# A spectral filter's time transform split as 128 by 16 points instead of 64 by 32, its middle matmuls in smaller array tiles

## The chip, the cores and the metric

The kernel runs on one core of a Trainium2 chip. The metric is the device time of one execution in microseconds (us); the figure given is the median of several runs. The engines are PE (TensorE matmul, with PEld its weight loads), DVE (VectorE), ACT (ScalarE), POOL (GpSimd) and SP (SyncE, which only issues transfers here).

## What is computed

The reference applies two blocks, and then both again. Block A normalises each row, takes a two-dimensional real Fourier transform over 2048 times and 512 features, multiplies it by a complex filter, transforms back and adds the input. Block B normalises, multiplies by two weight matrices, multiplies the two products elementwise, multiplies by a third matrix and adds the input.

```python
def _A_ref(x, w_r, w_i):
    X = rfft2(x, axes=(-2, -1))
    X = X * (w_r + 1j * w_i)
    return irfft2(X, s=(S, D), axes=(-2, -1))
def _B_ref(x, w_gate, w_up, w_down):
    return ((x @ w_gate) * (x @ w_up)) @ w_down
x = x + _A_ref(_layernorm(x), A_w_r, A_w_i)
x = x + _B_ref(_layernorm(x), B_w_gate, B_w_up, B_w_down)
```
The last two lines run twice: B=1, S=2048, D=512, F=1792.

## The kernel before, in words

The input lies in SBUF as `xs`, 128 partitions by 16 tiles by 512 features. Each of the two layers has three stages.

**Forward transform** (`fwd_rest`, from L459). Each of the 16 tiles is folded over the features, and four float32 matmuls into a PSUM bank `tp` do the long part of the time transform together with its twiddle factors (`tw`, from the constant `tf`). With 64 by 32 points a tile holds two of the 32 short indices, 64 rows each, so that half of every `tw` is zeros. ACT (or ACT and DVE) copies `tp` to `E`, which holds 4 blocks by 16 tiles by 16 groups by 8.

**Middle** (`middles`, L519, and `middle`, L549). The loop over `TWOS` (L1010) takes the 16 groups of frequencies in turn. For every group:
- `fs`: the sum and the difference of two halves of `E`, on POOL (on DVE for groups 0 and 1);
- `dp`: the transform over the features, 8 matmuls, each with 64 stationary columns of `fs` and 128 moving columns of `df`, written to one or the other half of the PSUM partitions; two groups share one planned step;
- `zs`: an ACT copy of `dp` to SBUF;
- `zp`: the short part of the time transform, 2 matmuls (4 in group 0) over all 128 partitions with 64 columns of a constant (`f2`, `f20`) each, and 512 moving columns;
- the filter, a complex product. Even groups go way "1": two ACT instructions put the swapped halves of `zp` in `jz`, DVE multiplies `zp`, POOL multiplies `jz`, DVE adds them to `ys`. Odd groups go way "2": four DVE instructions, with the swapped product in a PSUM bank `qp`;
- `vq`: the short part backward, 8 matmuls, each with 64 columns of `ys` stationary and 128 columns of a constant moving;
- an ACT copy of `vq` back into `E`.

**Inverse and product stages.** `inv` (L590) reads all 16 groups of `E`: its first matmuls `yi` wait for the last of these copies. Then the rows are normalised, turned and split into high and low parts (`build_x`), and the matmuls of block B (`gx`, `gw`, ..., `db`, `ex`, ...) follow.

Float32 matmuls leave two matmul and two weight load records each. The routine `halves` (L317) is what places two matmuls in the two column halves of the array:

```python
def halves(o, a, b):
    for c in (slice(0, 64), slice(64, 128)):
        TE.matmul(o[c], a[:, c], b, start=True, stop=True, skip_group_check=True)
```

The order on every engine is written out: `Plan.op` records each step with its engine, an assumed pitch and what it reads and writes, and `Plan.order` (L257) replays the steps in the order packed in the string `ORDER`, with places in the buffer rings from `PLACES`. Each engine runs its steps strictly in that order. All instructions are recorded through the queue wrapper, at L303. PSUM has eight banks: rings "x", "y", "w" of one, "a" of three and "d" of two (L224); SBUF temporaries such as `zs`, `jz` and `ys` share the ring "f" of 18. Before the middle and after it `idle` (L514) issues one 512-column matmul `wp` that nothing reads.

Of the kernel before, what the change touches and what calls it, by code (L numbers as in the profile page):

```python
# [14 lines left out]
ALU = mybir.AluOpType  # L15
# [13 lines left out]
def consts():  # L29
# [19 lines left out]
    j, p, q = np.arange(32), np.arange(64), np.arange(32)  # L49
    c, s = _cs(q[:, None, None] * (32 * p[None, :, None] + j[None, None, :]), 2048)  # L50
# [4 lines left out]
    tf = np.zeros((2, 64, 16, 16, 2, 2, 2))  # L55
    ti = np.zeros((64, 2, 16, 2, 64))
    for jj in range(2):
        tf[jj, :, :, :, :, jj] = f.reshape(16, 2, 2, 64, 16, 2)[..., jj].transpose(3, 4, 0, 2, 1)
        ti[:, jj, :, jj] = g.reshape(64, 64, 16, 2)[..., jj].transpose(0, 2, 1)
    w = np.exp(-2j * np.pi * (np.outer(j, j) % 32) / 32)  # L60
    late = np.exp(-1j * np.pi * j / 32)[:, None] * w
    unit = np.array([1.0, 1j])
    fs, gs = [], []
    for special in (False, True):
        z = np.zeros((2, 2, 32, 2, 32), complex)
        y = np.zeros((2, 2, 32, 2, 2, 32))
# [7 lines left out]
        fs.append(np.stack([z.real, z.imag], 3).reshape(2, 2, 16, 2, 128).transpose(0, 2, 1, 3, 4).reshape(128, 128))  # L74
# [10 lines left out]
        gs.append(y.reshape(128, 2, 2, 16, 2).transpose(0, 1, 3, 2, 4).reshape(128, 128) / 2048)  # L85
    mid = np.concatenate([*fs, *gs], 1).astype(np.float32)
# [16 lines left out]
SWAPS = "12" * 8, "12" * 8  # L103
FAST = (0, 1)
CUTS = {g: ((0, 12), (12, 16)) for g in range(3)}
TWOS = [(0,)] + [(g, g + 1) for g in range(1, 15, 2)] + [(15,)]
# [10 lines left out]
    'c-l=`2Y3}#)1GtgO%Dkz5a|*+ibyp<igZMpNReW}f_zf^M35>dRT2FJ73?4&iV#phP(Tncbiqc6h#(y)0YV5#_RRmz>?ZzCp1pVP*;A*y^UiFDqNzMZQ68V<+vq%(p|f0)u5m2g#C6UjIzus'  # L117
    '(NQVC8YG}W~<){RmV1t%QxUTaRu8i+%Xi30ajx)Iwe&6IuxX<Gl++V=6V)(p^)^aqJvYF%xEZPgW3dK=1Doy7&9y64{h+SNpLYV0kTg+XKEP7SOo(z?vEBLfnV;QH|G?&H0sVy_lH`81U)un'
    'j4f%zQHVbM$0Er}7w`C0s0hLL44uR#m5d{?FeTmy4E?7uWcqNOx`W%G3|jybkq4(94q5xc6Q>;BAlWByo3p$5fbrsI4KJ?qkT^t>G_T;lRNe-=m5LF~IcBw)~UKiAjx9h^*`VeNPt4JjvL#S'
    'pcot1P=@UaRZ1r{$bvpaZNG#&1h|&{lv^W%x4Hp}9N)t#9Mp=XfPQh*>@U6H<$zT%5vEGMV5{WMJqXT)*pGEHqr1e&Xgh+d8fa87{}lX%uVIJz04K`iM@W@Wj$@{3u<7WUg{e8o?9v{066dj'  # L120
    'yKXmoi7J_s)O&^lpgxsv3JA`rEOdfmSLbdS?>d$uBVHq!}xqc_feYu;-ipi9`0vAFTMqppaERK??HmM<J8yr63fXOQEQ$?rLf=U`5jn~fy52X<2P}41{PKV`@CQGGFK%f`jhWi+J}A(agz4D'
    '4O%mLdU=vUr`hN@hFyw956ABxcqdNN88*SZ3~lA<N3_;bJ2QHv@zeNx4A&(*Igjg3)w9ey*t`$_=!f6CSfu@jn`#DgY2F!X2DM#O30-y<s4477)?LHWcPIPfJE*R9K+gB5loHjxrLDBt$*EM'
    'Fc0&URXuE^t$$TAcpvQ(-dppZct6|;?cy@(5>a!3e_6>gozsli#u>OZA9jks$W1OXl<{%%z7^fc4m-?y{+F@Vf6P01#&1fjkN83{L5+4{upRn|nS=#{x;#CWgG@WN+#R$3u-#icPdEA4tRol'
    'b0|8(`nZFqK-k74CD@IC|i@8TSeRJ;8Ot9I4<bofO>d{>9|dvLBIMh~i~GHr`qL-{*8in%vnw@snN2e>~hH=R6pks5Lz^h;ph>a*w=iv(`RZkOua(~xxxP8QZR53$JpaasTm`UUORAfb)e=_'
    'fkgLay?;h*I>7`S9E(^d^slO+vHmYvwhY0~?N^dUP4B3-~#Vc$1^3xypV!r&CY97i$^l>=G{_=SEOnJD$3Di+CKpj`n8g`Jn4=U&Z}g9t$sd2jeY0kGtaNVQCaBYAW}F_Zw=AS@(O7*-<POU'
    'PAYh5LkRe-EoY`H#1F?H=$rFy<|3ErW$;JAE8;mYlmOgToi>&UrvXX1R2E+4{=?L&&B-?ubE}O<{~kxf#=^zd1$T0g7ya~3iJPp>zo^GzQ*@`be^_)Einb!xFSYWpfdET8)ME=8U9DDcfNP8'
    'ZHfCi-hVB00{{4h%Nj#9@a%j18bIH{J4^EgoU9V>(Q}2&89eDj!(AsU{$=40k?bhMtmt}_Z@Cy#jwK2;G@{3*l;igC8ux;Y0`kn|H*J;|hZSz4vKY77g{cMB+y_rLz><?Li82vs#8wWHc%D@'
    'mKIE;i+t8yMpXW$(Ol`Lc_4FRJ(NvFrr5R?Sxe8CdSNmshk{?6daaeaeJwzGsQj0w??}g<)NtuXVhgtTq8|M*y);8ivGTRj@iIwUbSvMW~yWgBsyQ&KNw2C|i=$b~UYFWOI%3lJ_=EigiUKF'
# [12 lines left out]
    'sRNdYb>NQ7QOxlp6%<_1Mig{qts?%k!Ov>_f&m4o^H4hIOR0`HIDj&&x$0XfY`FS#JdQU=SG&SKT&i4gFJ}}T!fKKuLI^Ti^v#P6!+S}W|pzw&q`&P*R?|6dr}mgb)}8us^3FfZ87EmTK~b-'
    '7P}MaYzuNY`D}nO)s!bS-~*U_8jW?Ynkjt4#hXGayp9~qM;XZ_-hlu8<GLF^>v#MMkB58=&UFTP%L97qaagsl3#ng}pxI`z`->*fYuo{zk)!hc+&yPj;%)-@jAOl?t39ny4jf7IT{qK7SI^`'
    '9e3B*mDW<3IK;I!V8wNHcBffM!O#&@*A0oQ1<GIw?r3CwKqvx&**;+_h<RhMVH}ca&$SXvCJ|DufG3@jIY?i3I)OE!SaWsZ}c5mPtvw_Ur%xbqK(BgPlsX>odk!`HfYRzTX`q%J?ii$OYJeG'
    'R9uZ<x87MA)>qGsj|fv&#B{Mfgjo9S*Jb|-Y-Va>Kr2eugvZJy-8?u_yEzC}mLS!Tl*cNbYi9nEaSt`h>^i-9MGgIYyZpkyu8d{}J+RsyCF4%o^p&8!NM=NE41TH9Md#5duG23gn!mOL-dt8'
    'b0QioNJRI<Sl_iVHs|dtArAdiPl0Z~oyjwAPzww{lA`sXOgv^k`iat9B|!mb}eJ&8@Jg@<^=CsEi`11>##N>?uN@rhBDqNO$Ucr0*g1wW=Uo$^boO_xmyX4Q4M+`NdXnbiaONky9Fa1X;WEe'
    '^BRG!M&k}Mw%ha@yc1hK4GX%Ad^G<tk-~sSwWs0oIg?bUP(WH5BP$Q2(^G5sev@4_VPFK#Ea0v4)#$-B%T7ipXe>YDo1o|gtlaARb(0+E0CzP8Bf<L7R$_;q9d(fh+iFKsSh<)PKP~$O&qe3'
    '%7g!aUkK)Afx$Kc>y*9M#Q0X2>lD{g-`a&fwPA0aFmAp59eeAD85?;&*xq>dH{Vb3-T|C63{MLKO)|j3cjMZiavtpMv@x{bG=MiJ!}1Csn=EK2nl?hWKg0Ip@Rtu15Dt*bR|>!faF!KjGpzG'
    '0cHh}cgZ=%>*d>CCWrtPLQMht6_c^LIa#<^znOa$>PChc03Tk)p`YF=s2`!xFazJdE<40)VPcG!%=Mc9fLp{V&#rqprA$dt0l~nc<6Cj_jy$}#Ua*<+19{C$swX}c3etvz4n^3yR@;brZWcF'
    '0L0-LxctcnMzz9oO$Zz{T2_{u17qK@!~XtmDn8XxY(98&wOr4?OaRl*bedd49x2@P#4%1$GdO(r3G9*w;856HPxQ0J09n>FT~)>vKzXq7;IrE;Ij>av~^kxsGRzdx>QM`FUy{Hx|Y6|`czhI'
    '<9pl%%L6m>~?YcYr$GfU%4-CIdfr<GYZRv<dt}80@0pewx-#{O9Wf--r!<rv~+5tE*(eqB4;AXW^2uB9C_z>7;fd&#nR~Q>AK!-_P;W%3{O7)ozf|E&c|QZ$|QaH1eruuyzwNihS|VZ5T4#q'  # L150
    '!{Pneh};_1ldHvVtt;niDiz5;jdvt!dTN7-nkE`ZAdD=tH3Fhn^0p~t-f0U2pghDwbDJFUI7X`Vw^jQ9A__2;y19P6_TkU63l?~AH;nxTEgv2bDqxW@N^5l9HyCC<4M%)+rVeuP|N6tcu)n`'
    '?TFxCWA-{MdwvhQeH=XS2uEwJ?iMtb1G^FKd7jq;S&l;2A>_ppdoysB7pX1}&=cfyU#$m9jU<ZvD(-Cj`UJoFOT9qr6L-K~_NtEVfhCCc7IQyXom0z-L*JHanH@E&T*^1JPbxfV7Z7O@{fBx'
# [120 lines left out]
def kernel(ctx: ExitStack, tc: tile.TileContext, x, wf, wc, wb, dfwd, tf, ti, mid, out):  # L273
# [245 lines left out]
    def middles(gs, E, df, W, due, swaps):  # L519
# [26 lines left out]
        for g, dp in zip(gs, dps):  # L546
            middle(g, dp, E, W, due(g), swaps[g])
# [620 lines left out]
```

## Time and profile before

| | |
|---|---|
| median of 3 runs | 1038.42 us (1037.62 to 1038.68) |
| the profiled execution's own time | 1037.49 us |
| its span | 1035.7 us |
| PE busy | 1020.6 us (99%) |
| DVE busy | 793.7 us (77%) |
| POOL busy | 745.8 us (72%) |
| ACT busy | 419.7 us (41%) |

The span is what the profiler saw from the first to the last instruction; the execution's own time is 1.8 us longer. Busy time is a sum over the whole span, and the stages differ: the profile by windows and the chain of waits tell which engine sets the pace in each.

### The profile page before, as it was taken

Reading aid. Unit: us, or ns where it says so; the run is one execution under the profiler, and the core shown is the slowest. Engines: PE = TensorE matmul, PEld = TensorE weight load, DVE = VectorE, ACT = ScalarE, POOL = GpSimd, SP = SyncE. Lnnn points to the kernel's source line nnn. Section 1 sums busy time; section 2 is a strip of 40 time slices with the busy share of each in tenths; the row PEclk is TensorE's granted clock in tenths of the full one; section 3 lists DMA queues with packets and bytes.
Section 4 is the critical chain, followed back from the end, with each engine's and each line's share of the span. In section 5 each row is a group of like instructions: output and inputs, shape, how many; then the busy total and the mean of one; then the engine's idle time right before and its main releaser. Section 6 shows DMA issues by size and latency. Waiting matters only on the chain.

```text
span 1035.7 us, 18681 instructions
## 1 busy us (share of the span) xinstructions
PE 1020.6 (99%) x6544; PEld 878.8 (85%) x6544; DVE 793.7 (77%) x1533; ACT 419.7 (41%) x989; POOL 745.8 (72%) x950
## 2 busy tenths in 40 slices
PE   8999999999999999999999999999999999999998
PEld 6777988888888888889987789888888888888897
DVE  7779777678866677778878796888887766677788
ACT  6679534434432422332376693222333421222231
POOL 6968999999997675655798466554779953456571
PEclk9999999999999999999999999999999999999999
DMA  9720677767785675455290005536796365565442
GB/s 346 304 80 19 225 241 237 251 186 254 221 272 185 211 253 188 152 203 206 87 386 10 9 5 207 202 123 220 217 255 198 103 205 191 204 244 204 153 142 82
DMA packets 129468, 193.65 MB, mean 187 GB/s; under 512 B 39264, under 2 KB 50784, under 8 KB 127328
## 3 DMA queue, kind: packets, MB, share of 16 engines
q1 hardware_dynamic: 129232, 192.21, 55.1%
q8 instruction: 52, 0.85, 0.3%
q14 instruction: 40, 0.33, 0.1%
q10 hardware_dynamic: 144, 0.26, 0.1%
HBM read 145.52 MB, written 46.92 MB: 186 GB/s over the span
## 4 chain that ended last, share of the span: by engine, by line
PE 93%; DVE 4%; DMA 1%; ACT 1%; issue 1%; POOL 1%; SPq 0%; DVEq 0%; ACTq 0%
PE gz L303 15%; PE gx L303 15%; PE db L303 8%; PE gw L303 7%; PE gy L303 7%; PE gv L303 7%; PE ex L303 5%; PE ez L303 5%; PE ew L303 3%; PE dp L303 3%; PE zp L303 3%; PE ev L303 3%; PE vq L303 3%; PE ey L303 3%; PE tp L303 3%; DVE xs L303 2%
## 5 line engine op out<-in xcount | busy, mean ns | idle before, releaser
L303 PE MATMUL gx<-xA,wt 128*128 128x512 f32 (+1 forms) x756 | 175.5, 368 | 0.0
L303 PEld LDWEIGHTS gx<-xA,wt 128*128 128x128 f32 x756 | 130.4, 189 | 21.3 <-ACT s L303 0.2
L303 POOL TENSOR_TENSOR sf<-q,sf 128x256 fp32r<-128x256 f32 x99 | 73.2, 744 | 84.4 <-ACT sf L303 79.9
L303 POOL TENSOR_TENSOR sf<-cc,sf 128x256 fp32r<-128x256 f32 x97 | 72.1, 745 | 57.5 <-ACT sf L303 57.3
L303 DVE TENSOR_TENSOR xs<-xs,db 128x512 f32<-128x512 f32 x128 | 85.0, 681 | 24.3 <-PE db L303 23.9
L303 PE MATMUL db<-wd,h 128*128 128x512 f32 x336 | 89.5, 392 | 0.1
L303 PE MATMUL gz<-xS,wt 128*128 128x512 f32 (+1 forms) x378 | 88.3, 369 | 0.0
L303 PE MATMUL gy<-xS,wt 128*128 128x512 f32 (+1 forms) x378 | 88.2, 369 | 0.1
L303 PE MATMUL gz<-xA,wt 128*128 128x512 f32 (+1 forms) x378 | 88.1, 369 | 0.0
L303 PE MATMUL gw<-xS,wt 128*128 128x512 f32 (+1 forms) x378 | 87.8, 368 | 0.0
L303 PE MATMUL gv<-xS,wt 128*128 128x512 f32 (+1 forms) x378 | 87.5, 367 | 0.0
L303 ACT CAST sf<-q 128x256 fp32r<-128x256 f32 x99 | 39.9, 406 | 101.5 <-DVE q L303 53.7
L303 PEld LDWEIGHTS gv<-xS,wt 128*128 128x128 f32 x378 | 65.5, 189 | 11.1 <-issue 0.2
L303 PEld LDWEIGHTS gw<-xS,wt 128*128 128x128 f32 x378 | 65.4, 189 | 10.9
L303 PEld LDWEIGHTS gz<-xA,wt 128*128 128x128 f32 x378 | 65.0, 189 | 10.5
L303 PEld LDWEIGHTS gz<-xS,wt 128*128 128x128 f32 x378 | 64.8, 189 | 10.6
L303 PEld LDWEIGHTS gy<-xS,wt 128*128 128x128 f32 x378 | 64.8, 189 | 10.6 <-DVE cc L303 0.3
L303 PEld LDWEIGHTS db<-wd,h 128*128 128x128 f32 x336 | 62.5, 188 | 13.2 <-DVE xs L303 0.5
L303 ACT COPY s<-gx 128x512 f32<-128x512 f32 (+1 forms) x63 | 33.8, 536 | 96.8 <-PE gx L303 93.7
L303 DVE TENSOR_TENSOR q<-gy,s 128x512 f32<-128x512 f32 (+1 forms) x63 | 39.7, 630 | 39.6 <-PE gy L303 24.3
L303 POOL TENSOR_TENSOR wt<-rg,wt 128x512 fp32r<-128x512 f32 (+1 forms) x56 | 64.3, 1155 | 3.8 <-ACT wt L303 3.8
L303 PEld LDWEIGHTS ez<-bf,sf 128*128 128x128 f32 x402 | 56.3, 190 | 5.2 <-issue 0.7
(166 smaller groups left out, 2486.1 us busy)
## 6 DMA issues: line engine op xcount, KB each, us to landing
wt<-gu SPq DMA_DIRECT2D x36, 1024.0 KB, 7.3
wt<-gu SPq DMA_DIRECT2D x36, 768.0 KB, 6.2
bf<-dn SPq DMA_DIRECT2D x20, 1024.0 KB, 5.5
wq<-in_wf_dram SPq DMA_DIRECT2D x16, 1024.0 KB, 8.5
bf<-dn SPq DMA_DIRECT2D x20, 768.0 KB, 4.7
gu<-wt SPq DMA_DIRECT2D x14, 1024.0 KB, 6.3
gu<-wt SPq DMA_DIRECT2D x14, 768.0 KB, 6.0
rg<-in_wb_dram SPq DMA_DIRECT2D x14, 512.0 KB, 4.3
```

The source lines that it names most:

```text
L303: ins = f(*args, **kw)
```

## The change

Three things change together, and the written order with them.

The split of the 2048 times becomes 128 by 16: one tile of `xs` holds 128 rows of one short index, `tf`, `ti`, `f2`, `f20`, `g2`, `g20` and the rows of the filter are laid out anew, and `tf` has no zero halves. The number and the shapes of the matmuls `tp`, `yi`, `yo` stay, and so do the sizes of all inputs.

The three matmul steps of the middle use smaller array tiles: `dp` and `vq` 16 matmuls a group, each 128 rows by 32 stationary columns, and `zp` for a pair of groups 16 matmuls, each 64 rows by 32 columns with 256 moving columns; the two row halves write to two PSUM banks.

The filter step runs over a pair of groups, all by way "3": two ACT instructions put the swapped halves in a PSUM bank `qp`, and DVE multiplies `zp`, multiplies `qp` in place, and adds. POOL has no part in it any more. Every `vq` reads both `ys` of its pair. The rings change too: all `dp` and `vq` take banks of ring "a", `zp` of "d" and "w", `qp` of "y" and "x". `TWOS` has one group to a step, and `ORDER` and `PLACES` are new strings for the whole kernel.

```diff
-SWAPS = "12" * 8, "12" * 8
+SWAPS = "3" * 16, "3" * 16
-TWOS = [(0,)] + [(g, g + 1) for g in range(1, 15, 2)] + [(15,)]
+TWOS = [(g,) for g in range(16)]
...
 def features():
-    for fs, dp in zip(fss, dps):
-        f4 = fs().rearrange("p j t (e q) -> p j (t e) q", q=2)
-        for q in range(2):
-            for j, c, odd in ((0, 0, 0), (2, 1, 0), (3, 0, 1), (1, 1, 1)):
-                o = 256 * q + 128 * odd
-                TE.matmul(dp()[64 * c:64 * c + 64, o:o + 128], f4[:, j, :, q], df()[:, j], ...)
-pe(0.83 * len(gs), features, ...)
+    f4 = fs().rearrange("p j t (e q) -> p j (t e) q", q=4)
+    for q in range(2):
+        for odd in range(2):
+            o = 256 * q + 128 * odd
+            for c in range(2):
+                j = (0, 2, 3, 1)[2 * odd + c]
+                for h in range(2):
+                    at = 64 * h + 32 * c
+                    TE.matmul(dp()[at:at + 32, o:o + 128], f4[:, j, :, 2 * h + q], df()[:, j], ..., tile_position=(0, at))
+pe(0.83, features, ...)
...
-def across():
-    if g:
-        halves(zp(), f2, zs())
-    else:
-        for q, m in enumerate((f20, f2)):
-            halves(zp()[:, 256 * q:256 * q + 256], m, zs()[:, 256 * q:256 * q + 256])
-pe(0.86, across, [zs, "midt"], [zp])
+def across():
+    for n, zs in enumerate(both):
+        o = 256 * n
+        for c in range(2):
+            for q in range(2):
+                for h in range(2):
+                    f = (f20 if m == n == h == q == 0 else f2)[64 * h:64 * h + 64, 32 * c:32 * c + 32]
+                    at = 64 * c + 32 * q
+                    TE.matmul(here[h]()[at:at + 32, o:o + 256], f, zs()[64 * h:64 * h + 64, 256 * q:256 * q + 256], ..., tile_position=(64 * h, at))
+pe(0.98, across, [*both, "midt"], here)
...
+if how == "3":
+    act(512, lambda qp=qp, zp=zp: A.mul(qp()[0:64], zp()[64:128], -1.0), [zp], [(qp, 0)], more=0.11)
+    act(512, lambda qp=qp, zp=zp: A.copy(qp()[64:128], zp()[0:64]), [zp], [(qp, 1)], more=0.11)
+    dve(512, lambda y=y, zp=zp, ri=ri: tt(y(), zp(), ri(0), ALU.mult), [(qp, 0), (qp, 1), zp, w], [y])
+    dve(512, lambda qp=qp, ri=ri: tt(qp(), qp(), ri(1), ALU.mult), [w], [(qp, 0), (qp, 1)])
...
+dve(512, lambda y=y, qp=qp: tt(y(), qp(), y(), ALU.add), [(qp, 0), (qp, 1)], [y])
+for g in (2 * m, 2 * m + 1):
+    last(g, ys, E, due(g))
...
 def back():
-    for q in range(2):
+    for h in range(2):
         for par in range(2):
-            o = 256 * q + 128 * par
-            halves(vq()[:, o:o + 128], y()[:, o:o + 128], g2 if g or q else g20)
+            o, at = 256 * h + 128 * par, 256 * (g % 2) + 128 * par
+            for c in range(0, 128, 32):
+                TE.matmul(vq()[c:c + 32, o:o + 128], ys[h]()[:, at + c:at + c + 32], g20 if g == h == 0 else g2, ..., tile_position=(0, c))
```

## Rows read from the trace of the kernel before

**Rows 1.** The page: busy time by engine, and the granted PE clock in 40 slices.
```profile
PE 1020.6 (99%) x6544; PEld 878.8 (85%) x6544; DVE 793.7 (77%) x1533; ACT 419.7 (41%) x989; POOL 745.8 (72%) x950
...
PEclk9999999999999999999999999999999999999999
```

**Rows 2.** Windows: middle of layer 0, middle of layer 1, and the stretch after each.
```profile
core 0: us, PE busy (x) PEld busy (x) DVE busy (x) ACT busy (x) POOL busy (x), PEclk, DMA share, GB/s
26.83:69.77 42.94, 42.94 (x583) 32.98 (x582) 32.33 (x51) 29.62 (x54) 37.24 (x51) 1.00 0.53 207
537.81:582.41 44.60, 43.18 (x583) 32.98 (x582) 32.82 (x50) 27.34 (x49) 30.15 (x44) 1.00 0.16 61
70.03:91.98 21.95, 19.94 (x123) 14.60 (x122) 19.69 (x62) 18.56 (x50) 18.21 (x23) 1.00 0.09 28
```

**Rows 3.** The chain that ended last, layer 0: start us, us, what.
```profile
26.90 2.77 PE dp L303 x48
...
46.51 1.75 PE dp L303 x32
48.25 1.72 PE zp L303 x8
49.97 0.87 PE vq L303 x16
...
63.90 5.24 PE vq L303 x96
69.14 1.06 PE wp L303 x2
70.19 2.68 PE yi L303 x24
```

**Rows 4.** The same chain, layer 1.
```profile
537.88 1.05 PE dp L303 x16
...
539.65 1.08 PE zp L303 x8
...
575.61 6.11 PE vq L303 x112
581.72 1.05 PE wp L303 x2
```

**Rows 5.** Groups by form in 26.83 to 69.77 us: busy, mean ns, idle before.
```profile
L303 POOL TENSOR_TENSOR jz<-jz,wq 128x512 f32<-128x512 f32 x8 | 10.2, 1280 | 0.9 <-POOL wt L303 0.7 <-ACT jz L303 0.2
L303 ACT COPY E<-vq 128x512 f32<-128x512 f32 x16 | 9.3, 587 | 5.4 <-PE vq L303 5.4
L303 DVE TENSOR_TENSOR ys<-qp,ys 128x512 f32<-128x512 f32 x8 | 5.5, 686 | 0.2
L303 ACT CAST wt<-rg 128x512 fp32r<-128x512 f32 x3 | 1.9, 625 | 0.0
```

**Rows 6.** ACT in order of time, layer 0 and layer 1: start, us, instruction.
```profile
28.03 0.58 ACT L303 COPY zs<-dp 128x512 f32<-128x512 f32 x1 [2.33 <-PE dp L303]
...
43.04 1.07 ACT L303 COPY E<-vq 128x512 f32<-128x512 f32 x2 [1.10 <-PE vq L303]
...
571.63 0.59 ACT L303 ACTIVATE jz<-zp 64x512 f32<-64x512 f32 x1
572.24 0.58 ACT L303 COPY jz<-zp 64x512 f32<-64x512 f32 x1
```

**Rows 7.** DVE in order of time, layer 0.
```profile
32.81 1.30 DVE L303 TENSOR_TENSOR zp<-zp,wq 128x512 f32<-128x512 f32 x2 [5.38 <-ACT jz L303]
...
36.09 0.67 DVE L303 TENSOR_TENSOR ys<-zp,wq 128x512 f32<-128x512 f32 x1
36.68 0.67 DVE L303 TENSOR_TENSOR ys<-zp,jz 128x512 f32<-128x512 f32 x1
...
66.45 0.70 DVE L303 TENSOR_TENSOR qp<-zp,wq 64x512 f32<-64x512 f32 x1
67.19 0.69 DVE L303 TENSOR_TENSOR ys<-qp,ys 128x512 f32<-128x512 f32 x1
```

**Rows 8.** Waits in 537.8 to 583 us: who waited, us in total, times, longest.
```profile
ACT jz L303 <- PE zp L303: 6.9, 7, 1.9
...
ACT zs L303 <- PE dp L303: 5.4, 7, 2.1
ACT E L303 <- PE vq L303: 4.9, 11, 1.2
```

More of the change, by code (lines that the diff above doesn't have):

```diff
@@ L54, in consts @@
     f[0, 1] = g[0, 1] = (1.0 - 2.0 * (p % 2))[:, None]
[L55 to L61, printed above, removed]
+    tf = f.reshape(16, 4, 2, 128, 16).transpose(3, 4, 0, 2, 1)
+    ti = g.reshape(128, 128, 16).transpose(0, 2, 1)
+    w = np.exp(-2j * np.pi * (np.outer(j, j) % 16) / 16)
+    late = np.exp(-1j * np.pi * j / 16)[:, None] * w
     unit = np.array([1.0, 1j])
@@ L64, in consts @@
     for special in (False, True):
-        z = np.zeros((2, 2, 32, 2, 32), complex)
-        y = np.zeros((2, 2, 32, 2, 2, 32))
+        z = np.zeros((2, 2, 16, 2, 16), complex)
+        y = np.zeros((2, 2, 16, 2, 2, 16))
         for cc in range(2):
@@ L84, in consts @@
                     y[ri, sg, :, 1, 0], y[ri, sg, :, 1, 1] = u.real, u.imag
-        gs.append(y.reshape(128, 2, 2, 16, 2).transpose(0, 1, 3, 2, 4).reshape(128, 128) / 2048)
-    mid = np.concatenate([*fs, *gs], 1).astype(np.float32)
+        gs.append(y.reshape(2, 32, 2, 2, 16).transpose(0, 1, 2, 4, 3) / 2048)
+    back = []
+    for first in (gs[0], gs[1]):
+        b = np.zeros((2, 2, 32, 2, 16, 2, 2))
+        for e, one in enumerate((first, gs[0])):
+            b[:, e, :, :, :, e] = one
+        back.append(b.reshape(128, 128))
+    mid = np.concatenate([*fs, *back, np.zeros((128, 128))], 1).astype(np.float32)
     single = lambda a: a.astype(np.float32)
@@ L349 @@
     midt = cp.tile([128, 512], F32, name="midt")
-    f2, f20, g2, g20 = (midt[:, 128 * i:128 * i + 128] for i in range(4))
+    f2, f20 = midt[:, 0:64], midt[:, 64:128]
+    g2, g20 = midt[:, 128:256], midt[:, 256:384]
     ident = cp.tile([128, 128], F32, name="ident")
@@ L533, in middles @@
             fss.append(fs)
[L534 removed]
+            dps.append(bank("dp", "a"))
+        (g,), (fs,), (dp,) = gs, fss, dps
         def features():
[L537 to L543 removed]
@@ L545, in middles @@
-        pe(0.83 * len(gs), features, [*((fs, i, lo) for g, fs in zip(gs, fss) for lo, _ in CUTS.get(g, ((0, 16),)) for i in range(2)), df, *(["idle"] if gs[0] == 0 else [])], dps)
-        for g, dp in zip(gs, dps):
-            middle(g, dp, E, W, due(g), swaps[g])
-    def middle(g, dp, E, W, due, swap):
+            f4 = fs().rearrange("p j t (e q) -> p j (t e) q", q=4)
[6 more added lines that the diff above has]
+                            at = 64 * h + 32 * c
+                            TE.matmul(dp()[at:at + 32, o:o + 128], f4[:, j, :, 2 * h + q], df()[:, j], start=True, stop=True,
+                                      skip_group_check=True, tile_position=(0, at))
@@ L550, in middle @@
+        pe(0.83, features, [*((fs, i, lo) for lo, _ in CUTS.get(g, ((0, 16),)) for i in range(2)), df, *(["idle"] if g == 0 else [])], [dp])
         zs = temp("zs", "f")
         act(512, lambda: A.copy(zs(), dp()), [dp], [zs])
-        zp = bank("zp", "da"[g % 2])
-        def across():
-            if g:
-                halves(zp(), f2, zs())
-            else:
-                for q, m in enumerate((f20, f2)):
-                    halves(zp()[:, 256 * q:256 * q + 256], m, zs()[:, 256 * q:256 * q + 256])
@@ L576, in middle, with spread @@
-        vq = bank("vq", "wd"[g % 2])
+        zss.append(zs)
+        if g % 2:
+            spread(g // 2, zss[-2:])
+            middle(g // 2, E, W, due, swaps)
+    zss, zps = [], [None, None]
+    def spread(m, both):
+        zps[:] = [bank("zp", "d"), bank("zp", "dw"[m % 2])]
+        here = list(zps)
+        def across():
+            for n, zs in enumerate(both):
[5 more added lines that the diff above has]
+                            at = 64 * c + 32 * q
+                            TE.matmul(here[h]()[at:at + 32, o:o + 256], f, zs()[64 * h:64 * h + 64, 256 * q:256 * q + 256],
+                                      start=True, stop=True, skip_group_check=True, tile_position=(64 * h, at))
+        pe(0.98, across, [*both, "midt"], here)
@@ new lines, in middle @@
+    def middle(m, E, W, due, swaps):
+        ys, w = [], W.key[m]
+        for h in range(2):
+            zp = zps[h]
+            ri = lambda i, h=h: W(2 * m + h, i)
+            y, how = temp("ys", "f"), swaps[2 * m + h]
+            ys.append(y)
+            if how == "1":
+                jz = temp("jz", "f")
+                act(512, lambda jz=jz, zp=zp: A.mul(jz()[0:64], zp()[64:128], -1.0), [zp], [(jz, 0)], more=0.11)
+                act(512, lambda jz=jz, zp=zp: A.copy(jz()[64:128], zp()[0:64]), [zp], [(jz, 1)], more=0.11)
+                dve(512, lambda zp=zp, ri=ri: tt(zp(), zp(), ri(0), ALU.mult), [(jz, 0), (jz, 1), w], [zp])
+                pool(512, lambda jz=jz, ri=ri: gtt(jz(), jz(), ri(1), ALU.mult), [w], [(jz, 0), (jz, 1)])
+                dve(512, lambda y=y, zp=zp, jz=jz: tt(y(), zp(), jz(), ALU.add), [zp, (jz, 0), (jz, 1)], [y])
+                continue
+            qp = bank("qp", "yx"[h])
+            if how == "3":
[3 more added lines that the diff above has]
+                dve(512, lambda qp=qp, ri=ri: tt(qp(), qp(), ri(1), ALU.mult), [w], [(qp, 0), (qp, 1)])
+            else:
+                dve(512, lambda y=y, zp=zp, ri=ri: tt(y(), zp(), ri(0), ALU.mult), [zp, w], [y])
+                dve(512, lambda qp=qp, zp=zp, ri=ri: stt(qp()[0:64], zp()[64:128], -1.0, ri(1)[64:128], op0=ALU.mult, op1=ALU.mult), [zp, w], [(qp, 0)])
+                dve(512, lambda qp=qp, zp=zp, ri=ri: tt(qp()[64:128], zp()[0:64], ri(1)[0:64], ALU.mult), [zp, w], [(qp, 1)])
+            dve(512, lambda y=y, qp=qp: tt(y(), qp(), y(), ALU.add), [(qp, 0), (qp, 1)], [y])
+        for g in (2 * m, 2 * m + 1):
+            last(g, ys, E, due(g))
@@ L578, in back, with last @@
+    def last(g, ys, E, due):
+        vq = bank("vq", "a")
         def back():
-            for q in range(2):
+            for h in range(2):
                 for par in range(2):
-                    o = 256 * q + 128 * par
-                    halves(vq()[:, o:o + 128], y()[:, o:o + 128], g2 if g or q else g20)
-        pe(0.92, back, [y, "midt"], [vq, *(["turn"] if g > 14 else [])])
+                    o, at = 256 * h + 128 * par, 256 * (g % 2) + 128 * par
+                    for c in range(0, 128, 32):
+                        TE.matmul(vq()[c:c + 32, o:o + 128], ys[h]()[:, at + c:at + c + 32], g20 if g == h == 0 else g2,
+                                  start=True, stop=True, skip_group_check=True, tile_position=(0, c))
+        pe(0.92, back, [*ys, "midt"], [vq, *(["turn"] if g > 14 else [])])
```

183 lines of the change are left out of this document (87 added, 96 removed).

## The prediction, made before the changed kernel was run

> **What bounds the kernel now.** Read the page first. PE is busy for 99% of the span and its granted clock is 1.0 throughout, the upper of its two levels, 2.4 GHz [rows 1]. A busy PE can still hide slack, so the chain of waits comes next. In the middle of layer 0 it runs over PE alone, from the first `dp` at 26.90 us to the last `vq` at 69.14 us; it ends with six `vq` in a row, work that PE had put off, and with the filler `wp` before `yi` [rows 3]. Layer 1 is the same with some waiting at its start [rows 4]. The windows say how near the other engines are: in 42.9 us of layer 0 DVE is busy for 32.3, ACT for 29.6 and POOL for 37.2; layer 1 takes 44.6 us, with PE waiting 1.4 of them [rows 2]. So the two middles are PE-bound, with DVE and ACT at about 70%. In the 22 us after the middle, PE, DVE and ACT are all near 19 us busy [rows 2]: that stretch starts when the last `vq` is back in `E`, and moves with it. What counts is when the last `E` copy lands: 69.77 and 582.41 us.
>
> **PE, now.** Two groups of `dp` take 1.75 us, so 0.875 a group; two of `zp` 1.72, so 0.86; one of `vq` 0.87 [rows 3]. That is 2.6 a group, 5.2 a pair and 41.7 a layer, the whole 42.2 us from 26.90 to 69.14.
>
> **PE, `dp` and `vq`.** Half the stationary columns and twice the matmuls: the moving columns double, and four array tiles can share them instead of two. If all four run side by side the price stays 0.875 and 0.87; if only two do, it doubles. The trace shows no four; it shows that two column halves do run side by side: `zp`, 4 records of 512 columns, takes 0.86 us a group, and the filler `wp`, with 2 records of the same columns in one tile, the same time but for 0.2 [rows 3]. I take the low end, the row of the same kind of split, and keep the other.
>
> **PE, `zp`.** For a pair 32 records of 256 columns in eight tiles: four rounds of 256 columns. The 8 records of 256 columns in two tiles (group 0, layer 1) are also four rounds, and took 1.08 us from a standing start [rows 4]; without the start it is 0.86, as for one group of 512. Low end 0.86 a pair against 1.72 now; high end two tiles at a time, 3.4. I take 0.86.
>
> **PE, change of shape.** Now all three steps share one shape. After the change each pair goes from 128 to 64 rows and back. The nearest rows are changes between 128 and 64 columns: `wp` after `vq` takes 1.06 and 1.05 us against the 0.86 of the same columns, so 0.2; the first `dp` after `wp` takes 1.05 against 0.875, so 0.18 [rows 3, 4]. Between nothing and 0.2 I take 0.18, twice a pair.
> The Trainium skill ("TensorEngine Tiling (Array Packing)", Key Properties) says that a change of tiling mode drains the engine while a change of tile doesn't, which speaks against this change; no row shows it for these shapes. By that rule the 32 changes cost 5.8 us in all, without it nothing.
>
> **PE, sum.** A pair is 2 x 0.875 + 2 x 0.87 + 0.86 + 0.36 = 4.71 us, a layer 37.7 against 41.7: 4.0 saved in each layer if PE stays the bound and idles no more than now.
>
> **ACT.** Back-to-back copies of `zs` and `E` start 0.48 us apart (two take 1.07, one 0.59), half swaps 0.61 apart (571.63 to 572.24) [rows 6]. Now a layer has 32 x 0.48 + 16 x 0.61 = 25.1 us. Way "3" swaps in every group: 32 x 0.48 + 32 x 0.61 = 34.9, or 4.36 a pair. That `qp` is now in PSUM may change the 0.61; no row shows ACT copying from PSUM to PSUM. I bound it by the 0.48 of a full copy and by 0.75, which is 0.61 made longer as DVE's 0.60 is by its `qp` instructions, 0.74 apart [rows 7]; I take 0.61, the row of the same instruction, and at 0.75 a layer would have 4.5 us more on ACT. ACT had idle time for this; it has hardly any after.
>
> **DVE and POOL.** DVE has 3 instructions a group, as now on average (2 in even groups, 4 in odd): 48 a layer, 0.60 to 0.74 us apart [rows 7], about 31 us. No gain and no loss. POOL loses 8 `jz` of 1.28, 10.2 us a layer [rows 5]; POOL isn't on the chain there, so nothing is gained but earlier `fs`. Laying out the constants, the filter and the rows anew leaves every transfer and every `tp`, `yi`, `yo` as it is: nothing. PE's instruction stream grows in the middles, about double for `dp` and `vq`; PE shows no wait for instructions in the chain now, and I put nothing.
>
> **The end of the middle, by the slowest path, layer 0.** Head: two `dp` from 26.90, the first `zs` at 28.03 [rows 6], both by 29.6, `zp` to 30.9 with its change of shape: ACT idles about 1.5. Until the last swap ACT has 16 `zs` (7.7), 32 swaps (19.5) and, if six `E` copies are put off as now, 10 copies (4.8): 32.0. The six copies and casts not of this stage lie in that window too (three `wt` casts are 1.9 [rows 5]); I count 1.0 of casts ahead. That is 28.0 + 1.5 + 32.0 + 1.0 = 62.5. Then come the last three DVE instructions (2.0), two `vq` (1.74, since both now wait for the pair), one copy (0.59) and some 0.2 for each of three hand-overs: 67.4. PE's path is 26.9 + 37.7 + 0.8 = 65.4; DVE's, from about where its first `zp` instruction stands now, 32.8 [rows 7], 32.8 + 31 + 2.7 = 66.5. ACT's is the longest: at best 2.4 earlier than 69.77.
> Layer 1 by the same steps from 538.95, without casts: 577.4 by ACT, 576.4 by PE, against 582.41: at best 5.0.
> Three paths within 2 us don't mesh without waiting. Each handover that is late holds up an engine with no slack; I allow 1.4 in layer 0 and 2.0 in layer 1, so 1.0 and 3.0 are left: **4.0 us**. The profiled execution (1037.49, its span and 1.8 around it) becomes 1033.5; the median of the runs stands 0.9 above that execution, so 1034.4.
>
> **Rivals.**
> *Everything meshes.* PE stays the bound in both layers: 2 x 4.0, 1030.4, and below 1030 if the change of shape is free. Against it: ACT's path is longer than PE's. Chance 0.08.
> *ACT eats the gain.* ACT waits more than I allow, and the end of the middles stays where it is: at 7.4/16 = 0.46 us of waiting a pair nothing is left, 1036.3 to 1040.5. For it: ACT now waits 6.9 us for `zp`, 5.4 for `dp` and 4.9 for `vq` in layer 1 [rows 8], though with time to spare. The Trainium skill (the same page, PSUM Bottleneck) warns that tiling speeds up TensorE and not the evacuation of PSUM; the sum above has that as ACT's path. Chance 0.21.
> *ACT sets a slower pace.* Place: the swaps of each pair, at the head of ACT's in-order queue, waiting for `zp`, with the `zs` of the next groups and the `E` copies behind them; PE then waits for `zs` and for banks of ring "a". A swap that waits now waits 0.99 us (6.9 in 7 times) [rows 8]. Once a pair, that is 16 x 0.99 = 15.8 against the 7.4 that there is to lose: 8.4 slower, 1046.8; at three quarters of it 1042.9. It decides from 0.46 a pair; against it, the swaps of two groups come together, so one wait serves four. Chance 0.13.
> *The tiles don't run side by side as the code says.* At two at a time `dp` and `vq` cost 0.87 more each, 64 of them 55.7 us, and `zp` 16 x 1.7 = 27: 1110 or more; if only the row halves of `zp` take turns, 16 x 0.86 = 13.8 more on PE, some 5 us slower than now. Against it: the two column halves run side by side in full today [rows 3]. Chance 0.06.
>
> **How the numbers follow.** The forecast, 1034.4, has 0.52; its own range is 1031 to 1036.3. A difference of 0.2%, about 2.1 us, is what a measurement can tell from none: faster is forecast and full meshing, 0.60; within it, ACT eating the gain, 0.21; slower, the last two, 0.19. The range runs from 1029.5 (the full PE gain) to 1042 (waiting of up to 0.7 us a pair) and leaves out the doubled `dp` and the worst of ACT.
>
> **What would show it.** `dp` and `vq` in the chain at 0.87 to 0.88 a group, `zp` at 1.1 to 1.3 a pair with its changes of shape; ACT busy some 9 us more in each middle and its share above 85%; no `jz` on POOL; the last `E` copy at about 68.8 and 579.4; everything behind it moved by the same amount, and the product stages as long as now. Wrong would be: PE steps at other prices, `zs` or `E` copies that hold up PE with a middle as long as before, or a difference that arises behind the middles, where I expect none.

## The result, and the profile after

| | before | after |
|---|---|---|
| median of the runs | 1037.64 us (1037.46 to 1038.68, 6 runs) | 1042.34 us (1039.36 to 1046.04, 6 runs) |
| the profiled execution's own time | 1037.49 us | 1039.36 us |
| its span | 1035.7 us | 1037.5 us |

The ratio after to before is 1.0045, with a 95% interval from 1.0024 to 1.0066: the changed kernel is slower by about 0.45%, where 1034.4 us was forecast, 0.3% faster. Two things stand beside the median: the runs of the changed kernel spread over 6.7 us, those of before over 1.2, and the profiled execution is the fastest of its six. So its trace accounts for 1.9 of the 4.7 us by which the medians differ; the rest lies in executions that have no trace.

The page of the changed kernel answers to [rows 1]. The first and last lines here are its busy times and the queue that brings PE's instructions (its packets are the ones that grow with PE's records): packets, MB and share of 16 DMA engines.

```profile
PE 1015.0 (98%) x7944; PEld 876.6 (84%) x7944; DVE 790.8 (76%) x1533; ACT 433.8 (42%) x1021; POOL 726.9 (70%) x934
...
PEclk9999999999999999999999999999999999999999
...
q8 instruction: 63, 1.03, 0.4%
```

PE works 5.6 us less than before, at the same granted clock, and the kernel is longer. PE's records grow by 1400 matmuls and 1400 weight loads. The page of before has 52 packets on the instruction queue, so 2800 more records brought 11 more packets of 16.3 KB (1.03 MB over 63): about 255 instructions each. Such a packet is called a block here.

The windows of the two middles, from the first `dp` to the last `vq`, and of the stretch after layer 0's, answer to [rows 2]; the columns are the same.

```profile
26.60:73.57 46.97, 40.12 (x1282) 31.87 (x1281) 31.30 (x49) 36.45 (x69) 28.47 (x45) 1.00 0.41 164
542.40:583.75 41.35, 38.73 (x1282) 31.75 (x1281) 31.53 (x52) 34.74 (x64) 20.50 (x37) 1.00 0.21 79
74.50:96.40 21.90, 19.87 (x122) 14.47 (x122) 19.56 (x63) 18.25 (x50) 18.88 (x24) 1.00 0.55 195
```

PE is busy for 40.12 us of 46.97 in layer 0: it idles 6.85 us, where it idled not at all [rows 2]. The windows of before end with the last `E` copy, 0.6 us behind the last `vq`; from the first `dp` to the last `vq` layer 0 takes 46.91 us against 42.24, and layer 1 became shorter, 41.34 against 43.84. The stretch behind (21.90 us against 21.95) only moves. So the question is what PE waits for in the middles, and the chain of waits says it. Layer 0, against [rows 3]: start, us, what.

```profile
26.66 2.33 PE dp L312 x75
28.99 2.46 issue
31.46 0.89 PE dp L312 x21
...
35.50 0.65 PE zp L312 x10
36.15 1.33 issue
37.47 1.06 PE zp L312 x22
...
41.32 0.31 PE vq L312 x9
41.63 1.71 issue
43.34 0.86 PE vq L312 x23
...
74.63 1.45 PE yi L312 x12
```

"issue" is time in which an engine waited for nothing that the profile shows. Three of them, 5.50 us, stand on PE, and each cuts a step in two: 75 of a run of 96 records of `dp`, 10 of 32 of `zp`, 9 of 32 of `vq`. How much PE does between two stalls says what they have in common. The windows from the end of one stall to the start of the next:

```profile
31.46:36.15 4.69, 4.46 (x127) 3.03 (x128) 1.36 (x3) 3.47 (x7) 4.69 (x9) 1.00 1.02 421
37.47:41.63 4.16, 4.16 (x127) 3.48 (x127) 2.98 (x5) 2.74 (x5) 1.75 (x3) 1.00 1.02 423
```

127 matmul and 128 weight load records, then 127 and 127: each time one block of instructions, whatever step it ends in. The first `yi` comes at 74.63 us, 4.44 later than before. Layer 1, against [rows 4]:

```profile
542.41 2.85 PE dp L312 x96
...
546.28 2.34 PE dp L312 x78
548.62 1.45 issue
550.08 0.82 PE dp L312 x18
...
562.58 1.02 PE zp L312 x32
563.61 1.91 PE dp L312 x64
565.52 1.08 PE vq L312 x32
...
584.80 1.23 PE yi L312 x11
```

One more of the same kind, 1.45 us, so PE's stalls are 6.95 us in all. (Gaps of 0.46 us at 552.63 and 0.48 at 571.66, the second of which the expectations below count in their 7.4 us, stand between instructions of ACT, and PE works through them.) From first `dp` to first `yi` layer 0 takes 47.97 us (43.29 before), layer 1 42.39 (44.90): 4.68 lost and 2.51 won. As the first middle began 0.24 us earlier, `yi` of layer 1 is 2.0 us late, and the span has grown by 1.8.

What PE waits for is seen on the DMA queues. The first two blocks of lines are the queues of the changed kernel from 20 to 29 us and from 29 to 30.2 us (packets, MB, share of 16 engines); q1 carries the data, q8 PE's instructions.

```profile
q1 hardware_dynamic: 1049, 3.61, 100.7%
q14 instruction: 1, 0.01, 0.2%
...
q1 hardware_dynamic: 75, 0.49, 99.9%
q8 instruction: 1, 0.02, 5.0%
```

For the 9 us up to the stall no block of instructions comes, while the data queue fills every engine. One comes in the window 29 to 30.2, and takes 5.0% of 16 engines over 1.2 us, so 0.96 us of one; it starts at 29.16, and PE goes on at 31.46. The blocks ahead of the other three stalls' ends start at 35.09, 41.02 and 547.75 us and take as long, and PE goes on at 37.47, 43.34 and 550.08: each time 1.3 to 1.4 us after the block's end. Before, the same window from 20 to 29 us holds one block, although the data queue is just as full:

```profile
q1 hardware_dynamic: 878, 3.61, 99.1%
q8 instruction: 1, 0.02, 0.7%
```

The data is the filter: seven transfers of 1 MB to `wq`, issued from 19.8 to 29.1 us, and it moves at some 375 to 450 GB/s until 43 us. After that no stall of a microsecond is left in layer 0.

### The profile page after: what moved, and what is told of

It is laid out like the page before. It is cut to its first block, busy times and chain, and to the rows that moved or that the text cites. A ratio compares the mean times of both kernels' runs of the same rounds, so it can differ in the third digit from the quotient of the medians.

```text
span 1037.5 us, 21515 instructions
## 1 busy us (share of the span) xinstructions
PE 1015.0 (98%) x7944; PEld 876.6 (84%) x7944; DVE 790.8 (76%) x1533; ACT 433.8 (42%) x1021; POOL 726.9 (70%) x934
## 3 DMA queue, kind: packets, MB, share of 16 engines
q8 instruction: 63, 1.03, 0.4%
## 4 chain that ended last, share of the span: by engine, by line
PE 90%; DVE 5%; issue 1%; ACT 1%; DMA 1%; POOL 0%; DVEq 0%; ACTq 0%; POOLq 0%
PE gz L312 15%; PE gx L312 15%; PE db L312 8%; PE gw L312 7%; PE gy L312 7%; PE gv L312 7%; PE ez L312 5%; PE ex L312 5%; PE ew L312 3%; PE ev L312 3%; PE ey L312 3%; PE dp L312 2%; PE vq L312 2%; DVE xs L312 2%; PE yi L312 2%; PE zp L312 2%
## 5 line engine op out<-in xcount | busy, mean ns | idle before, releaser
L312 POOL TENSOR_TENSOR sf<-q,sf 128x256 fp32r<-128x256 f32 x104 | 77.0, 745 | 94.0 <-ACT sf L312 89.7
```

The lines of the kernel that those rows point to most:

```text
L312: ins = f(*args, **kw)
```

## The experiments

Theory 1, formed from these rows: **PE runs out of instructions**, because the new matmul shapes take about twice as many of them in the same time, and the blocks that bring them are late beside the filter's transfers. Rival: the stalls belong to the new tiles themselves (their data, their banks or their shape) and would stand there with an idle DMA. The Theory 2 of the expectations below is another rival: ACT's queue sets the pace of the middles. Kernels of before on the same chips had medians of 1037.1 to 1037.6 us.

**Small filter, on both kernels.** Seven of the eight filter transfers are cut to an eighth; all pairs use part 0. The edit on the changed kernel, and the same on the kernel before:

```diff
+cut = slice(0, 32) if n else slice(0, 256)
-load(1024, lambda: SP.dma_start(self.part(n), wf[:, n]), ...
+load(1024, lambda: SP.dma_start(self.part(n)[:, :, :, cut], wf[:, n, :, :, cut]), ...
-return self.part(g // 2)[...]
+return self.part(0)[...]
```

> The changed kernel, but of the eight filter parts of a layer only the first is loaded whole (1 MB); of the other seven an eighth is loaded, and all pairs are multiplied by the first part. It leaves out seven eighths of the filter and 6 MB of transfers beside each middle; no engine has an instruction less. Theory 1 (PE runs out of instructions because its instruction blocks land late beside the filter loads): the gaps of 2.46, 1.33, 1.71, 1.45 and 0.48 us in PE's chain that have no releaser go, the last E copies come some 3 to 5 us earlier in layer 0 and 1 to 2 in layer 1, and the time falls by 4 to 7 us, to 1034 to 1037, with runs within 1 us of each other. Theory 2 (ACT's queue sets the pace of the middles): ACT has the same work, the gaps move elsewhere, and the time stays at 1040 to 1043.

> The kernel before with the same cut of the filter loads, as the control: it leaves out seven eighths of the filter. Both theories: its PE shows no such gaps now, so within 1 us of 1037.6. If it falls by 3 us or more, the filter loads cost something else, and the first run says nothing on instructions.

Measured: the changed kernel takes 1034.14 us (1033.33 to 1034.76), ratio to before 0.9966 [0.9953, 0.9979]; the kernel before 1037.30, ratio 0.9997 [0.9988, 1.0006]. Taking away transfers is worth 8 us to the changed kernel and nothing to the one before. The chain of the changed kernel with the small filter, both layers:

```profile
26.78 2.33 PE dp L312 x75
29.11 0.54 issue
29.66 0.89 PE dp L312 x21
...
537.04 2.42 PE dp L312 x80
539.46 1.35 issue
540.81 0.68 PE dp L312 x16
...
579.66 1.45 PE yi L312 x13
```

The break in `dp` is at the same 75th record, with 0.54 us in place of 2.46; the stalls at 36 and 41 us are gone. One of 1.35 us stays in layer 1: the filter is not all that is moved there (1 MB goes to `bf` just ahead). The tiles, the banks and the engines' work, ACT's too, are those of the changed kernel, so both rivals fall.

**Dense instructions, on the kernel before.** The other half of the theory: double the instructions and leave all else.

```diff
 def halves(o, a, b):
-    for c in (slice(0, 64), slice(64, 128)):
-        TE.matmul(o[c], a[:, c], b, ...)
+    for c in range(0, 128, 32):
+        TE.matmul(o[c:c + 32], a[:, c:c + 32], b, ..., tile_position=(0, c))
```

`zp` and `vq` go through this routine, and `dp` is cut in the same way.

> The kernel before with its old split, old filter step and old order, but every dp, zp and vq matmul cut into two of 32 stationary columns: the same arithmetic and the same columns per array tile, twice the instructions in the middles. Theory 1: PE's steps keep their prices (dp 0.875 a group, vq 0.87, zp 0.86), but gaps without a releaser of 1 us or more appear between 27 and 50 us, and in layer 1; 2 to 7 us slower, 1040 to 1045. Theory 2: ACT, DVE and POOL have the work of before, so within 1 us of 1037.6.

Measured: 1039.38 us (1038.62 to 1040.49, 10 runs), ratio 1.0017 [1.0008, 1.0027]. The direction is the theory's, the size just below what was expected (1040 to 1045). Its chain in layer 0:

```profile
45.28 1.10 issue
46.39 1.84 PE vq L303 x60
```

A stall of 1.10 us inside `vq` appears where before had none, and the first `yi` comes at 72.03 us, 1.84 later. The prices of the steps are those of before. So density alone makes a stall, a smaller one than the change's. The written orders differ too: this one reaches its blocks at other moments, and issues the last filter transfer at 39.6 us (in the trace of before), the changed kernel at 29.1. What that order adds was not tested by itself.

**Fewer instructions in one step.** `vq` as four whole-array matmuls a group, everything else as changed:

```diff
-for c in range(0, 128, 32):
-    TE.matmul(vq()[c:c + 32, o:o + 128], ys[h]()[:, at + c:at + c + 32], ...
+TE.matmul(vq()[:, o:o + 128], ys[h]()[:, at:at + 128], ...
```

> The changed kernel with vq as 4 whole-array matmuls of 128 stationary columns a group in place of 16 of 32: the same columns streamed, 48 instructions fewer a group, 30% of the middle's. Theory 1: the first gaps lie before any vq and stay (2.46 and 1.33 us); the later ones shrink; against that stands one more change of array shape a pair, 16 x 0.18 = 2.9 us. Between 1038 and 1043. Theory 2: vq's shape is not ACT's concern, so 1040 to 1044, with the gaps where they are.

Measured: 1042.83 us, ratio 1.0048 [1.0033, 1.0063], no gain; both theories allowed that. The first stall, 2.75 us at 28.80, lies ahead of any `vq`, again behind the 75th record of `dp`; PE stands 0.87 us later on and, in layer 1, 1.90 and 1.37: 6.9 us in all, as in the changed kernel, though 57 blocks come in place of 63. Two groups of `vq` take 1.98 us against 1.75 to 1.86. Thinning one step of three does not shorten the waiting: the first block is late for a step that was not thinned.

**Spreading the filter.** If the 8 MB burst is the trouble, hold the transfers back: a one-column write by DVE in a part, after a multiplication of an earlier pair, lets its transfer go, and POOL's small correction of a part comes just ahead of its use; the result is the same. One run has them two pairs ahead, another three.

```diff
+y["fn"] = lambda: (run(), V.memset(self.part(m + LEAD)[:, 0, 0, 0:1], 0.0))
```

> The changed kernel with all of its filter, but the loads spread over the middle: the parts for pairs 2 to 7 are issued one by one, each held back until DVE has started on the pair two before it (a one-column clear of the part, 6 a layer, makes the transfer wait), and POOL's small correction of each part comes just ahead of its use. Nothing is left out. Theory 1: with one load in flight at a time the instruction blocks land in time, the gaps after the first go, the first shrinks to the 0.5 us of the run with the small filter; 1034 to 1036.5, faster than the kernel before by 0.1 to 0.35%. It costs DVE 6 x 0.06 us a layer. Theory 2 (ACT's pace): the gaps without a releaser turn into others, 1040 to 1043. If parts land late, DVE waits for POOL's correction and the middles grow: 1040 or more with DVE waiting on wq.

> The same with each part held back until DVE has started on the pair three before it, so that one load more goes out ahead of the middle. Theory 1: some of the gaps near 29 to 36 us come back, as more load is in flight there: between the run before it and the changed kernel, 1034.5 to 1038. If late parts were what limits the run before it, this one is the faster of the two.

Measured: 1044.52 us (1036.69 to 1053.44, 12 runs, the longest not in the ratio), ratio 1.0056 [1.0039, 1.0073], and 1045.01 (1039.59 to 1046.55, 6 runs), ratio 1.0061 [1.0042, 1.0079]. Both missed. The chain of the first shows why; three of its seven stalls:

```profile
38.66 0.67 issue
...
43.35 1.44 issue
...
59.11 1.91 issue
```

With the transfers spread out, there is now a stall in nearly every pair, up to 65 us: a single transfer of 1 MB beside a block is enough. In layer 1 one of 1.35 us is left, and small ones.

**Smaller packets.** The filter laid out so that its transfers go in packets of 2 KB or 512 bytes in place of 8 KB:

```diff
+wf = wf.reshape(128, 8, 4, 512).transpose(1, 2, 0, 3)
-SP.dma_start(self.part(n), wf[:, n])
+SP.dma_start(self.part(n).rearrange(...), wf[n].rearrange("b p f -> p b f"))
```

> The changed kernel with the filter laid out in device memory so that every filter transfer goes in packets of 2 KB in place of 8 KB; the bytes, their order and their time of issue stay. Theory 1a (an instruction block waits behind the data packets that are queued ahead of it, so its delay goes with the size of a packet): the stalls of PE in both middles shrink to well under half of the 7.4 us, first matmuls yi near 70 and 581 us, time 1035 to 1038.5. Rival (the delay goes with the bytes in flight, whatever their packets): stalls of 2.5, 1.3, 1.7 and 1.4 us as in the changed kernel, time 1041 to 1043. A second rival: smaller packets make the filter loads themselves slower, so that DVE waits for the filter; then the wait shows at DVE's first multiplications, and the time is above 1043.

> As the run with 2 KB packets, but with packets of 512 bytes. Theory 1a: stalls smaller again or gone, time 1034 to 1037, unless the loads become slower by more than they are early; rival (bytes in flight): 1041 to 1043; second rival (smaller packets slow the loads): the filter parts land late and the time is above that of the run with 2 KB packets, by some us in layer 0, where the loads fill the DMA engines.

Measured: 1042.58 us, ratio 1.0051 [1.0034, 1.0067], its largest stalls 1.71, 1.99 and, in layer 1, 1.92 us; and 1041.22, ratio 1.0037 [1.0025, 1.0049], with 1.88, 1.62 and 2.11. PE's stalls add up to 7.6 and 7.3 us, against 6.95 in the changed kernel. Theory 1a falls: what a block waits doesn't shrink with the size of single packets.

**Fewer bytes.** The two partition halves of the filter are equal, so half of it can be loaded and copied by POOL.

```diff
+SP.dma_start(self.part(n)[0:64], wf[0:64, n]) if n in HALF else SP.dma_start(self.part(n), wf[:, n])
...
+G.tensor_copy(self.part(n)[64:128], self.part(n)[0:64])
```

> The changed kernel with half the bytes in six of the eight filter transfers: partitions 64 to 127 of the filter hold the same values as partitions 0 to 63, so for pairs 2 to 7 only the lower half is loaded and POOL copies it to the upper half, after the first ys of the pair before; the result is the same. Theory 1b (an instruction block is late by the bytes that are in flight beside it): the loads of the middle shrink from 8 to 5 MB and end some 7 us earlier, the stalls of PE in both middles shrink from 7.4 us to some 3 us in sum, and the time would be 1036 to 1039. Rival (POOL becomes the bound): a copy of 64 partitions by 2048 columns is no row of the trace; at POOL's 0.73 us for 256 columns of two operands it would be up to 5.8 us, above what a pair of groups leaves (4.7 us less four fs of 0.73), so fs comes late: dp waits for POOL, time 1043 to 1055.

> As the run before it, but only the transfers of pairs 2, 4 and 6 are halved and copied: 6.5 MB in place of 8. Theory 1b: the stalls of PE in both middles shrink from 7.4 to some 5 us, time 1038 to 1041; if POOL is the bound in the run with six copies, half as many cost half or nothing here, as POOL can be ahead. Rival (POOL the bound): 1041 to 1046.

Measured: 1051.26 us, ratio 1.0133 [1.0117, 1.0149], and 1048.53, ratio 1.0115 [1.0096, 1.0135]: worse, and not for the rival's reason. POOL's copy takes 1.89 us, not the feared 5.8, and stands in no wait of note. The chain of the first run:

```profile
26.75 2.33 PE dp L323 x75
29.08 5.48 issue
34.57 1.51 PE dp L323 x21
...
40.87 0.57 PE zp L323 x10
41.44 2.71 issue
```

The same two places, the 75th record of `dp` and the 10th of `zp`, now with 5.48 and 2.71 us; in layer 1 a stall of 3.82. The stalls are not the whole loss. The window between the first two holds one block of PE's instructions again, and the third column from the end is the granted clock:

```profile
34.57:41.44 6.87, 6.87 (x127) 4.38 (x128) 1.99 (x3) 3.47 (x7) 3.17 (x3) 0.60 1.05 204
```

Behind each of the three stalls the granted clock is at 0.50, the lower level (1.2 GHz), for some microseconds, and the steps take longer: 21 records of `dp` 1.51 us in place of 0.89, 96 after the second stall 4.81 in place of 2.79. Its DMA queues from 28 to 40 us:

```profile
DMA packets 534, 2.49 MB, mean 207 GB/s; under 512 B 86, under 2 KB 173, under 8 KB 301
...
q1 hardware_dynamic: 532, 2.46, 101.1%
q8 instruction: 1, 0.02, 0.7%
```

A transfer into 64 partitions moved at half the rate here: 207 GB/s with all engines full, where the changed kernel moves 422 GB/s (30.2 to 35 us). Half the bytes take as long, and in 12 us a single block comes through. Theory 1b, that the bytes alone count, falls with it. What fits these runs is the time that the transfers already queued still take; it is not shown by itself.

**Quarters, held back.** So the spread transfers are cut into four of 256 KB, each let go by its own DVE multiplication:

```diff
+V.memset(self.part(m + LEAD)[cut][:, 0, 0:1], 0.0)
+SP.dma_start(self.part(m + LEAD)[cut], wf[:, m + LEAD][cut])
```

> The changed kernel with the filter loads of pairs 2 to 7 spread over the middle as in the run e5, but each cut into four transfers of 256 KB, one let go after each of four DVE multiplications of the pair two before, so that at most some 0.7 us of transfer (256 KB at about 400 GB/s) stands in the queues at a time. Theory 1c (an instruction block starts only when the transfers that are already queued ahead of it have ended): with at most 0.7 us ahead of it no block is late inside the middle of layer 0; what is left is the stall at 28.8 us (the loads of the start), some 1.5 us, and 1.4 us in layer 1; first yi near 70 to 71 and 580 to 581 us, time 1034.5 to 1037.5. Rival (any load that is in flight delays a block by several us, whatever stands ahead of it): the stalls of e5 stay, six of 0.7 to 1.9 us, time 1042 to 1046.

Measured: 1040.32 us (1037.25 to 1043.73, 12 runs), ratio 1.0024 [1.0012, 1.0035]; 4 us better than whole transfers, still above the range expected. In the profiled execution, with 1043.73 us as long as any of these, the stalls of PE in layer 0 are 2.47, 0.89, 0.80 and 0.18 us: shorter than with 1 MB transfers, but there; and behind the first the granted clock is 0.50 (31.59 to 34.50 us). In that trace POOL also stood 12.7 us for filter parts, so a last run moved the correction that waits for them to DVE:

```diff
-ad = pool(8, lambda: gtt(...
+ad = (dve if n >= LEAD else pool)(8, lambda: (tt if n >= LEAD else gtt)(...
```

> As e11 (filter loads of pairs 2 to 7 in quarters, held back), but the small correction of the filter parts 2 to 7 is made by DVE, just before the pair's first multiplication, in place of POOL, which in e11 stood 12.7 us waiting for filter parts, three times, with the fs of later groups queued behind. Theory: what is left of e11's loss in the first middle is the stall at the start (2.5 us at 29.1, whose block stands behind the loads of the start), three of 0.8 to 1 us, and POOL's standing; without the last, first yi near 72 to 73.5 and a time of 1037 to 1039.5. Rival: POOL's standing was hidden, the stalls alone set the time: 1039.5 to 1042, as e11.

Measured: 1040.63 us (1036.95 to 1043.37, 12 runs), ratio 1.0024 [1.0012, 1.0037]: POOL's standing was hidden, as the rival had it. What is new is the profiled execution, one of the short ones with 1037.62 us. Its chain has no stall at 29 us, and its queues from 20 to 29 us show why:

```profile
26.38 2.79 PE dp L321 x96
...
48.19 0.21 PE vq L321 x7
48.40 0.46 issue
```

```profile
q1 hardware_dynamic: 1201, 3.20, 91.1%
q8 instruction: 2, 0.03, 1.4%
```

Two blocks start before 29 us. The run of e11, whose chain stops for 2.47 us at 29.13, has none in the same window:

```profile
q1 hardware_dynamic: 1221, 3.38, 96.0%
q14 instruction: 1, 0.01, 0.2%
```

These two executions are 6.1 us apart, 5.45 of it at the first `yi` (75.17 and 69.72). They are executions of two kernels, which differ in the engine of the correction; but the runs of each spread as far (1037.25 to 1043.73 and 1036.95 to 1043.37).

The traces of all the kernels with the new middle say it together. Where the first block starts at 24.28 us (this run) or 25.05 (packets of 2 KB), `dp` isn't cut. Where it starts at 27.05 (small filter), 27.69 (512 bytes), 27.93 (spread), 29.16 (the changed kernel) and 31.58 us (half the bytes), the stall behind the 75th record is 0.54, 0.55, 1.65, 2.46 and 5.48 us: the later the block, the longer the stall. The other four, with 29.10 to 30.96 us and stalls of 2.47 to 4.66, fit in between. That it is this block, and the lower clock behind its stall, that spreads the runs of the changed kernel over 6.7 us is likely from these traces, but not shown for each run; three of the six have a mean granted clock of 0.997 or 0.998, the others 1.0, among them one of 1043.09 us.

No version that computes the same beats the kernel before by its median. With the small filter in both kernels, the new middle is worth 3.2 us (1034.14 against 1037.30), with 0.54 and 1.35 us of stalls still in it; a way to bring filter and instructions in time was not found.

## Why the prediction was wrong

**The step that failed** is the one on PE's instructions: "PE's instruction stream grows in the middles, about double for `dp` and `vq`; PE shows no wait for instructions in the chain now, and I put nothing." It measured 5.50 us of stalls in layer 0 and 1.45 in layer 1. That the chain of before shows no such wait says only that the blocks come in time at the rate of before: the instruction queue already shared full DMA engines then, in [rows 2] with 207 GB/s as a mean over a middle that has its filter loads at its start. At twice the rate the same delay is too long. The trace held a warning: instruction packets are counted on the page, and from 26 to 44 us the DMA share is 0.89 to 1.06. It held no row of a late block, so the price could not be read from it; but the term could have been bounded like the other unknown costs, and not put at nothing.

**What held.** The price of a pair on PE was put at 4.71 us. Where instructions come in time it is 1.02 for `zp`, 1.91 for two groups of `dp` and 1.75 to 1.86 for two of `vq`, 4.68 to 4.79 in all. So four column tiles do run side by side, as the row of two was taken to say. The changes of shape cost 0.16 where `dp` follows `zp` (1.91 against 1.75) and 0.16 in `zp` (1.02 against 0.86, if that is its price without the change), near the 0.18 taken; this agrees with the rule of the Trainium skill ("TensorEngine Tiling (Array Packing)", Key Properties) that a change of mode drains the engine.

ACT's swaps start 0.61 us apart, as taken (65.86 and 66.47 us in the chain of layer 0), also with both operands in PSUM, and ACT is busy 6.8 and 7.4 us more in the two middles, against some 9; its share is 78% and 84%, where above 85% was looked for. DVE is as busy as before (31.30 and 31.53 us against 32.33 and 32.82), POOL 8.8 us less in layer 0. Nothing arises behind the middles: from the first `yi` of layer 0 to the first `dp` of layer 1 it is 467.78 us against 467.69.

**The end of the middles.** The forecast was 1.0 us earlier after layer 0 and 3.0 more in layer 1. With the small filter the first `yi` comes at 69.18 us in layer 0, 1.01 earlier, and in layer 1 at 579.66, 3.12 earlier in all; so layer 1 gave 2.1, with a stall of 1.35 still in it. So the forecast's direction and paths hold for a kernel whose instructions arrive. That its time, 1034.14 us, lies so near the forecast 1034.4 is in part luck: the middles gave 3.1 us and not 4.0, and the profiled execution took 1034.76 where 1033.5 was forecast. The 0.9 us added for the median came from three runs; in six the median of before stands 0.15 above its profiled execution.

**The rivals.** The measured time lies just below where "ACT sets a slower pace" was looked for (1042.9 to 1046.8), but that is not what happened: the swaps are a small part of the chain (`qp` 6.9% from 26 to 76 us), and the long gaps stand inside PE's steps. No rival had this mechanism, so that the time lies near one of them is chance. The 1042.34 us is 0.3 above the range, which was built on ACT's waits.

**The page that bore on it** is in the Trainium skill ("Runtime: NRT & Kernel Launch", Instruction fetch mechanics): every engine streams its instructions in blocks of 16 KiB, 256 instructions, through a DMA queue of its own, into a small buffer, and a crossing is mostly hidden. The trace agrees on the block (16.3 KB, about 255 instructions) and on the queue. On the hiding it agrees for most of the 63 blocks of the changed kernel, but not for four, which cost PE 1.33 to 2.46 us each, and one beside slow transfers cost 5.48.

## What to carry to other kernels

When a change cuts matmuls into smaller tiles, count its instructions in each stage as well as its columns, and look at what the DMA engines do in that stage: instructions come over the same engines. An "issue" gap on PE that breaks a step in its middle, at the same record in several kernels and one block (here 254 or 255 records) behind the gap before it, is the sign of late instructions; check that PE itself is idle in it; to test for it, shrink the data transfers beside it on the new and on the old kernel. A spread of run times that grows with a change is a sign worth a look of its own: the fastest execution, which happened to be profiled here, hides most of the loss.

## What the runs showed of the hardware that was not expected

- The delay of an instruction block went neither with the packet size of the transfers beside it (8 KB, 2 KB and 512 bytes: 1042.34, 1042.58 and 1041.22 us) nor with their bytes (half the bytes at half the rate: stalls of 5.48 and 2.71 us). The stalls shrank with transfers that are short in time (256 KB each: 1040.32 us against 1044.52 with 1 MB). How the queues are served, and on which of the engines a block waits, no run here shows.
- PE goes on some time after its block is in: 1.3 to 1.4 us after the end of the block in all four stalls of the changed kernel.
- A stall of PE can cost twice. Behind the stalls of 5.48, 2.71 and 3.82 us the granted clock was 0.50 for some microseconds, and behind one of 2.47 us in the run with quarters too; in the profiled execution of the changed kernel it stayed at 1.00 behind 2.46 us.
- A transfer into 64 of the 128 partitions ran at half the rate, 207 GB/s against 422, with all 16 engines busy in both.
- POOL copies 64 partitions by 2048 float32 in 1.89 us, far below what its 0.73 us for 256 columns of two operands would give (5.8).
